# Up to eight MLP tiles ahead of their second matmul, kept in the spectral buffers while these are free, and three after that; the opening's order on two engines written out to tile 10; the splits of w2 placed among the other work

## The chip, the cores and the metric

The kernel runs on one core of a Trainium2 chip. The metric is the device time of one execution in microseconds (us). The core has a matmul engine (PE; its weight loads are PEld), a vector engine (DVE), a scalar engine (ACT), a general engine (POOL) and a queue that issues the DMAs (SP). Each engine works through its own list of instructions in order and waits at an instruction until what that one needs is there.

## The reference, cut to what is computed

```python
x = A_x                                        # [1, 2048, 512]
xn = layernorm(x, axis=-1)
X = rfft2(xn, axes=(-2, -1)) * (w_r + 1j*w_i)  # 2048 x 257 weights
y = irfft2(X, s=(2048, 512))
h = einsum("bsd,df->bsf", xn, w1) + b1         # 512 -> 1792
act = h * tanh(softplus(h))                    # Mish
return x + y + einsum("bsf,fd->bsd", act, w2)  # 1792 -> 512
```

All is float32. The kernel keeps that precision by splitting each float32 operand into a float16 "high" and "low" part and making three float16 matmuls of each product (high-high, high-low, low-high).

## The kernel before

**Two streams of work.** The MLP is cut into 4 groups `g` of 512 rows and 14 tiles `f` of 128 hidden columns. A tile goes *up* (`mlp_up`, L707: 12 matmuls into `ph_g_f`; ACT makes `hb` = Mish of it; then `split` makes the tile `a_g_f` in two halves, the high one on ACT and the low one on DVE) and *down* (`mlp_down`, L734: 12 matmuls `pa` with the tile `a_g_f` and the part f//2 of w2). Each up and each down is one *half-tile*; there are 112. After the last down of a group `mlp_end` adds x to the four sums (DVE `m`, L757; x comes by the DMAs `xr`, two at a time). The spectral branch is a 2-D transform over 16 sub-tiles `s2` = 4g+s of 128 rows, forward, times the weights, and back. `mlp_all` is a generator: `b(n)` takes the next n half-tiles from it and so lays MLP work between pieces of the other branch.

**The opening** (up to `spread`) loads x, w1, w2, normalises group 0, measures and splits w1 (seven parts, `split_w1`), measures w2 (`norm_w2`, seven parts; parts 0 to 2 on ACT, 3 to 6 on DVE) and sums these over partitions on POOL (`w2_scale`), which gives the scale for `split_w2`. Part c of w2 is split in place: it is written into block c and read from block c+1, so part c+1 can be split only after part c.

**The spread** (L913 to L956) then runs 21 slots. In a slot stand pieces of the spectral branch and then one `b(1)`. For groups 1 to 3 the pieces are `stats` (DVE statistics; then the reciprocal root `rs` by 14 small operations on POOL), `norm` (DVE `xs`; ACT high part of `xh`; POOL low part of `xh`), `transpose` (PE `pt`, 4 matmuls on the high and 4 on the low part, copied out by DVE and ACT to `xnT`) and `s1_forward` (PE `psS1`, three matmuls; ACT `bc`; DVE `bt` twice; ACT high and POOL low part of `y1`; DMA to `d_y1`). From slot 13 on, `prep_spectral` also loads the spectral weights once (`wm`) to find their largest value (DVE `mxw`). Of w2 one part is split in every second slot.

**After that** `stream_a` runs the second stage of the forward transform (`psP`), the spectrum (`psD`), and the way back (`psA`, a round trip by DMA through `d_a`, `psT`) for four chunks, with half-tiles laid between by weight up to half-tile 100; then `s1_inverse` (`psY`) with the last 12 half-tiles.

**What sets the order.** The code is recorded; a scheduler of the framework then orders each engine's list from the recorded dependencies and its own estimates. `tc.issue_after` and `in_order` add dependencies that only order. `behind()` puts pieces after the last up's and down's instructions.

**Buffers.** Each tag is a ring. Tiles `a` have a ring of 3, so a tile waits until the tile three before it in the ring has gone down; in group 0 the tiles 3 to 10 lie instead in the buffers "z" and "u" (four tiles each), which before held parts of w1 and later hold spectral data. `hb` has a ring of 3; `ph` and `pt` share a ring of 2 PSUM banks (tag "h"); `psS1` has 2 banks, `pa` 4; `bt`, `bc` and `xs` have 2, `y1` 3, `xh` 4 and the large load buffers ("big") 5.

`LAG`, `E_UP` and the condition in `mlp_all` (L767) set how far ups run ahead of downs: 11 ups first, then an up only when fewer than 2 tiles are ahead, or after two downs.

## Time and profile before

| | us |
|---|---|
| three runs, median | 422.77 (422.55 to 424.7) |
| the profiled execution, its own time | 423.4 |
| its span, first to last instruction | 421.6 |

The profiled execution's time is 1.8 us more than its span. In the profile a time is counted from the span's start; a row of a group gives busy time, the mean of one, and the idle time of the engine just before it with what ended it. "PEclk" is the share of full speed at which PE's clock ran. The mean of one matmul (383 ns for 512 columns) is longer than the distance of two that follow each other, since they overlap.

### The profile page before, as it was taken

The page shows a single profiled execution, that of the slowest core. Times are in us where ns is not written, and L with a number is a line of the kernel's source. Part 1 is how long each engine was busy: PE and PEld are TensorE (multiplying, and loading weights), DVE is VectorE, ACT ScalarE, POOL GpSimd, SP SyncE. Part 2 cuts the span into 40 slices and gives each one's busy share as a digit, 9 for nine tenths or more (in the row PEclk, how much of TensorE's full clock was granted, in tenths as well). Part 3 has the DMA queues.
Part 4 walks back from the last instruction along what each step waited for, and adds up shares of the span by engine and source line. Part 5 has one row for each costly group of instructions (what it writes and reads, how often), then busy time and mean ns, then how long its engine had stood idle before and what let it go on. Part 6 is the DMA issues. An engine that isn't in the chain of part 4 may idle for free.

```text
span 421.6 us, 6597 instructions
## 1 busy us (share of the span) xinstructions
PE 391.7 (93%) x2485; PEld 193.2 (46%) x2485; DVE 251.2 (60%) x520; ACT 202.1 (48%) x325; POOL 70.7 (17%) x103
## 2 busy tenths in 40 slices
PE   8889987999959799979999998999999899989996
PEld 3434333444424345445545464444555454543442
DVE  5979957872296313983495743776245955333435
ACT  4869737662244124644536453546435455342120
POOL 0000075874055100000112000111001120031000
PEclk9999998999997899989999999999999999999999
DMA  8995122353063994154514816315435111445675
GB/s 286 368 398 223 52 67 82 101 157 119 1 233 120 242 231 151 33 130 110 181 51 151 220 31 177 122 54 147 104 81 172 50 50 51 129 148 174 200 241 206
DMA packets 50816, 61.61 MB, mean 146 GB/s; under 512 B 3921, under 2 KB 36177, under 8 KB 50529
## 3 DMA queue, kind: packets, MB, share of 16 engines
q1 hardware_dynamic: 50784, 61.20, 47.6%
q8 instruction: 19, 0.31, 0.3%
q14 instruction: 13, 0.10, 0.1%
HBM read 44.38 MB, written 16.78 MB: 145 GB/s over the span
## 4 chain that ended last, share of the span: by engine, by line
PE 48%; DVE 15%; issue 10%; DMA 10%; ACT 7%; POOL 5%; SPq 4%; POOLq 0%; DVEq 0%; ACTq 0%
PE ph L716 18%; PE pa L87 6%; PE pa L83 6%; PE pa L86 6%; DMA ai<-d_a 3%; PE psP L512 3%; PE psD L536 2%; DMA cTt<-in_cT_dram 2%; DMA xr<-in_x_dram 2%; DVE m L757 1%; SPq L358 1%; ACT a L331 1%; DMA d_a<-at 1%; DVE w2r L332 1%; POOL y L126 1%
## 5 line engine op out<-in xcount | busy, mean ns | idle before, releaser
L716 PE MATMUL ph<-xnT,w1t 128*128 128x512 f16 x672 | 157.2, 383 | 2.4 <-ACT hb L721 2.3
L716 PEld LDWEIGHTS <-w1t 128*128 128x128 f16 x672 | 64.9, 99 | 80.1 <-issue 7.0
L83 PE MATMUL pa<-w2r,a 128*128 128x512 f16 x224 | 86.3, 386 | 3.4 <-DVE m L757 3.4
L87 PE MATMUL pa<-w2r,a 128*128 128x512 f16 x224 | 86.7, 387 | 2.0 <-DVE a L332 2.0
L86 PE MATMUL pa<-w2r,a 128*128 128x512 f16 x224 | 86.6, 387 | 1.0 <-DVE w2r L332 1.0
L332 DVE SCALAR_TENSOR_TENSOR a<-hb,sc_a,a 128x512 f16<-128x512 f32 x56 | 42.8, 767 | 72.2 <-ACT a L331 72.0
L721 ACT ACTIVATE hb<-ph,b1t,sc_exp 128x512 f32<-128x512 f32 x56 | 43.2, 773 | 69.9 <-PE ph L716 69.9
L126 POOL TENSOR_TENSOR tt<-bt_t,tt 128x512 f16<-128x512 f32 x16 | 19.2, 1206 | 216.1 <-DMA d_a<-at 115.7
L331 ACT ACTIVATE a<-hb,sc_a 128x512 f16<-128x512 f32 x56 | 40.1, 719 | 14.2 <-PE pa L87 13.0
L87 PEld LDWEIGHTS <-a 128*128 128x128 f16 x224 | 22.3, 99 | 31.2 <-issue 3.5
L86 PEld LDWEIGHTS <-a 128*128 128x128 f16 x224 | 22.3, 99 | 29.8 <-issue 6.7
L83 PEld LDWEIGHTS <-a 128*128 128x128 f16 x224 | 22.1, 99 | 25.8 <-issue 1.7
L126 POOL TENSOR_TENSOR y<-bt_s,y 128x512 f16<-128x512 f32 x16 | 20.2, 1266 | 30.0 <-ACT y L125 30.0
L331 ACT ACTIVATE u<-r,sc_u 128x512 f16<-128x512 f32 x16 | 11.6, 722 | 24.6 <-DVE r L616 13.8
L197 PE MATMUL pt<-cMt,xh 128*128 128x128 f16 x128 | 11.8, 225 | 10.8 <-ACT xh L190 3.4
L125 ACT CAST tt<-bt_t 128x512 f16<-128x512 f32 x16 | 9.9, 618 | 15.1 <-DVE bt_t L123 14.2
L805 DVE SCALAR_TENSOR_TENSOR m<-psY,sc_k,m 128x512 f32<-128x512 f32 x12 | 8.6, 747 | 14.2 <-PE psY L87 14.2
L197 PEld LDWEIGHTS <-xh 128*128 128x128 f16 x128 | 8.3, 99 | 18.5 <-ACT xh L190 5.3
L671 DVE SCALAR_TENSOR_TENSOR at<-psA,at 128x512 f16<-128x512 f32 x16 | 10.7, 686 | 8.9 <-ACT at L670 8.9
L525 DVE SCALAR_TENSOR_TENSOR z<-psP,z 128x512 f16<-128x512 f32 x16 | 10.8, 688 | 8.8 <-ACT z L524 8.6
L122 DVE SCALAR_TENSOR_TENSOR bt_t<-psT,bc_t 128x256 f32<-128x256 f32 x16 | 6.8, 423 | 14.0 <-ACT bc_t L118 12.6
L524 ACT ACTIVATE z<-psP 128x512 f16<-128x512 f32 x16 | 9.3, 593 | 11.9 <-PE psP L512 11.6
(146 smaller groups left out, 526.5 us busy)
## 6 DMA issues: line engine op xcount, KB each, us to landing
wt<-in_wt_dram SPq DMA_DIRECT2D x32, 256.0 KB
x<-in_x_dram SPq DMA_DIRECT2D x8, 512.0 KB
d_y<-y SPq DMA_DIRECT2D x16, 256.0 KB
wm<-in_wt_dram SPq DMA_DIRECT2D x8, 512.0 KB
yt<-d_y SPq DMA_DIRECT2D x16, 256.0 KB
d_a<-at SPq DMA_DIRECT2D x32, 128.0 KB
ai<-d_a SPq DMA_DIRECT2D x16, 256.0 KB
d_t<-tt SPq DMA_DIRECT2D x16, 256.0 KB
```

The lines of the kernel that those rows point to most:

```text
L83: first = nc.tensor.matmul(ps, stat(0), mov(0), start=start, stop=False)
L86: nc.tensor.matmul(ps, stat(0), mov(1), start=False, stop=False)
L87: return nc.tensor.matmul(ps, stat(1), mov(0), start=False, stop=stop)
L126: nc.gpsimd.tensor_sub(out[:, :, 1, :], tv, out[:, :, 0, :])
L197: nc.tensor.transpose(pt[:, h, dc, :], xh[:, h, dc * P : (dc + 1) * P], ident)
L331: hi = nc.scalar.activation(dst_h, src, AF.Copy, scale=scale)
L332: lo = nc.vector.scalar_tensor_tensor(dst_l, src, scale, dst_h, op0=ALU.mult, op1=ALU.subtract)
L512: first = nc.tensor.matmul(ps[64 * be : 64 * be + 64, pr, k, :], yt[:, 2 * pr + be, hs, k, :], c_p2[:, k, v, hm, :], start=t == 0, stop=t ...
L525: nc.vector.scalar_tensor_tensor(zl, psv, 2.0**-15, zh, op0=ALU.mult, op1=ALU.subtract)
L671: nc.vector.scalar_tensor_tensor(at[:, :, 1, :], psv, 2.0**-15, at[:, :, 0, :], op0=ALU.mult, op1=ALU.subtract)
L716: last_mm = nc.tensor.matmul(ph, w1t[:, hs, dc, f * P : (f + 1) * P], xnT[g][:, hm, dc, :], start=n == 0, stop=n == 11)
L721: nc.scalar.activation(hb, ph, AF.Mish, bias=b1t[:, f : f + 1], scale=s_exp[k])
```

## The change

It does this:

- **Lead.** While `sc["ahead"]` is set (until slot 15), an up is taken when fewer than 8 tiles are ahead (`LEAD`); after that when fewer than 3 are (`LAG` was 2). The first 11 ups stay. New conditions (`home`, `free`) let an up be recorded only if its buffer's earlier tile has gone down.
- **Where tiles lie.** Tiles are counted through (14g+f). Of each twelve, four lie in the ring `a` (now 4) and eight in "z" and "u", as long as `ahead` holds; before, these two took tiles 3 to 10 of group 0 only.
- **hb.** The ring is 2 (was 3); the first two tiles use the ring of `xs`.
- **Opening.** Tiles 0 and 1 are split later, together with tile 2. ACT's and DVE's order is written out by `in_order` from `bias_max` to tile 10. `norm_w2` 3 to 6 stand earlier, and `split_w2(0)` stands in the opening.
- **Spread.** Parts 1 to 6 of w2 stand in slots 1, 4, 7, 10, 13 and 15, first in the slot. There are 24 slots; `wm` loads run two steps ahead of their `mxw`.

```diff
-LAG = 2
+LAG = 3
+LEAD = 8
...
-        for c in range(8):
-            t = big.tile([P, 1024], F32, tag="big", name=f"wm_{c}")
-            nc.sync.dma_start(t, wt_any[:, 1024 * c : 1024 * c + 1024])
-            nc.vector.tensor_reduce(mxw[:, c : c + 1], t, axis=AX.X, op=ALU.max, apply_absolute_value=True)
+        wm = []
+        for c in range(10):
+            if c < 8:
+                wm.append(big.tile([P, 1024], F32, tag="big", name=f"wm_{c}"))
+                nc.sync.dma_start(wm[c], wt_any[:, 1024 * c : 1024 * c + 1024])
+            if c > 1:
+                nc.vector.tensor_reduce(
+                    mxw[:, c - 2 : c - 1], wm[c - 2], axis=AX.X, op=ALU.max, apply_absolute_value=True
+                )
...
-        hb = mp.tile([P, 512], F32, tag="hb", name=f"hb_{g}_{f}", bufs=3)
+        if g == 0 and f < 2:
+            hb = tp.tile([P, 512], F32, tag="ix", name=f"hb_{g}_{f}", bufs=2)
+        else:
+            hb = mp.tile([P, 512], F32, tag="hb", name=f"hb_{g}_{f}", bufs=2)
...
-        if g == 0 and 2 < f < E_UP:
-
-            if f in (3, 7):
-                sc["ea"] = tp.tile([P, 4, 2, 512], F16, tag="zu"[f // 4], name=f"a_{g}_{f}")
-            a = sc["ea"][:, (f - 3) % 4]
+        r = (NFC * g + f) % 12
+        if sc["ahead"] and r > 3:
+
+            if r % 4 == 0:
+                sc["ea"] = tp.tile([P, 4, 2, 512], F16, tag="zu"[r // 8], name=f"a_{g}_{f}")
+            a = sc["ea"][:, r % 4]
         else:
-            a = mp.tile([P, 2, 512], F16, tag="a", name=f"a_{g}_{f}", bufs=3)
+            a = mp.tile([P, 2, 512], F16, tag="a", name=f"a_{g}_{f}", bufs=4)
+            in_a.append(NFC * g + f)
         acts[g, f] = a
-        last["up"] = (last_mm.ins, *split(a[:, 0, :], a[:, 1, :], hb, sc["a"]))
+        wait.append((a, hb))
+        if g == 0 and f < 2:
+            return
+        if g == 0 and f in (2, 3):
+            split_w1(f)
+        while wait:
+            a, hb = wait.pop(0)
+            last["up"] = (last_mm.ins, *split(a[:, 0, :], a[:, 1, :], hb, sc["a"]))
...
-            if up < len(tiles) and (up < E_UP or up - down < LAG or (n_down == 2 and up - down > LAG)):
+            lag = LEAD if sc["ahead"] else LAG
+
+            home = sc["ahead"] and up % 12 > 3
+            free = down >= up - up % 4 - 8 if home else len(in_a) < 4 or in_a[-4] < down
+            if free and up < len(tiles) and (up < E_UP or up - down < lag or (n_down >= 2 and up - down > lag)):
...
-    with tc.issue_after(ends[0]), tc.issue_after(ends[1]):
+    with tc.issue_after(ends[0]), tc.issue_after(ends[1]), in_order(mybir.EngineType.Activation, mybir.EngineType.DVE):
+
...
-    b(2)
-    split_w1(2)
-    with behind():
-        norm_w2(0)
...
+        b(4)
+        norm_w2(3)
+        norm_w2(4)
+        b(1)
+        split_w1(4)
+        norm_w2(5)
+        b(1)
         norm_w2(0)
...
+        split_w2(0)
+        b(1)
+        split_w1(6)
+        b(1)
...
-        if w2_left and done[0] % 2:
-            split_w2(w2_left.pop(0))
...
+    for c in range(1, 7):
+        slots[(1, 4, 7, 10, 13, 15)[c - 1]].insert(0, (split_w2, c))
+
+    for k in range(13, 23):
+        slots[k].append((next, maxima, None))
     for k in sorted(slots):
+        if k == 15:
+            sc["ahead"] = False
```

**Place 1: ACT in the opening**, between the first two Mish tiles (`hb_0_0`, `hb_0_1`) and the tile `a_0_3`. In the rows `w1t<-w1s` is a part of w1 being split and `w2r,q2` a `norm_w2`. Before, and then with the change:

```order
L721 ACTIVATE hb_0_1_370<-ph_0_1_357,b1t_94,sc_exp_0_252 128x512
L331 ACTIVATE w1t_92<-w1s_2_106,sc_w1_1_325 128x4x256
L331 ACTIVATE a_0_0_354<-hb_0_0_352,sc_a_337 128x512
L331 ACTIVATE a_0_1_372<-hb_0_1_370,sc_a_337 128x512
L428 ACTIVATE w2r_93,q2_95<-w2r_93 128x1024
L721 ACTIVATE hb_0_2_391<-ph_0_2_378,b1t_94,sc_exp_0_252 128x512
L331 ACTIVATE w1t_92<-w1s_2_106,sc_w1_1_325 128x4x256
L331 ACTIVATE a_0_2_393<-hb_0_2_391,sc_a_337 128x512
L721 ACTIVATE hb_0_3_413<-ph_0_3_400,b1t_94,sc_exp_0_252 128x512
L331 ACTIVATE w1t_92<-w1s_4_109,sc_w1_1_325 128x4x256
L331 ACTIVATE a_0_3_415<-hb_0_3_413,sc_a_337 128x512
```

```order
L731 ACTIVATE hb_0_1_368<-ph_0_1_355,b1t_94,sc_exp_0_252 128x512
L731 ACTIVATE hb_0_2_384<-ph_0_2_371,b1t_94,sc_exp_0_252 128x512
L332 ACTIVATE w1t_92<-w1s_2_106,sc_w1_1_325 128x4x256
L332 ACTIVATE a_0_0_354<-hb_0_0_352,sc_a_337 128x512
L332 ACTIVATE a_0_1_370<-hb_0_1_368,sc_a_337 128x512
L332 ACTIVATE a_0_2_386<-hb_0_2_384,sc_a_337 128x512
L731 ACTIVATE hb_0_3_408<-ph_0_3_395,b1t_94,sc_exp_0_252 128x512
L332 ACTIVATE w1t_92<-w1s_2_106,sc_w1_1_325 128x4x256
L332 ACTIVATE a_0_3_410<-hb_0_3_408,sc_a_337 128x512
L731 ACTIVATE hb_0_4_432<-ph_0_4_419,b1t_94,sc_exp_1_327 128x512
```

`hb_0_2` moved ahead of the first part of w1, and the `norm_w2` that stood ahead of it moved further back (behind `a_0_5`).

**Place 2: DVE around the statistics of group 1** (`BN_STATS`, then `ve`), after the last of the first eleven tiles; `w2r<-w2r` is a `split_w2`, `qt`, `pn` and `sc_w2` are the small operations of `w2_scale`. Before, and then with the change:

```order
L173 BN_STATS st_1_530<-x_1_0_122 128x6
L317 TENSOR_SCALAR qt_w2_483<-qt_w2_483 128x1
L173 BN_STATS st_1_530<-x_1_0_122 128x6
L319 TENSOR_SCALAR pn_w2_487<-qt_w2_483 128x1
L173 BN_STATS st_1_530<-x_1_1_124 128x6
L325 TENSOR_SCALAR sc_w2_489<-pn_w2_487 128x1
L439 SCALAR_TENSOR_TENSOR s_out_491<-p2_H_335,pn_w2_487 128x1
L173 BN_STATS st_1_530<-x_1_1_124 128x6
L175 BN_AGGR mv_1_531<-st_1_530 128x2 x4
L332 SCALAR_TENSOR_TENSOR a_0_7_508<-hb_0_9_582,sc_a_337,a_0_7_508 128x512
L177 TENSOR_SCALAR ve_1_540<-mv_1_531 128x4
L332 SCALAR_TENSOR_TENSOR w2r_93<-w2r_93,sc_w2_489 128x1024
```

```order
L333 SCALAR_TENSOR_TENSOR w2r_93<-w2r_93,sc_w2_525 128x1024
L333 SCALAR_TENSOR_TENSOR a_0_8_514<-hb_0_9_544,sc_a_337,a_0_8_514 128x512
L333 SCALAR_TENSOR_TENSOR w1t_92<-w1s_6_112,sc_w1_1_325,w1t_92 128x4x256
L333 SCALAR_TENSOR_TENSOR a_0_8_514<-hb_0_10_563,sc_a_337,a_0_8_514 128x512
L174 BN_STATS st_1_567<-x_1_0_122 128x6 x2
L174 BN_STATS st_1_567<-x_1_1_124 128x6 x2
L176 BN_AGGR mv_1_568<-st_1_567 128x2 x4
L333 SCALAR_TENSOR_TENSOR w2r_93<-w2r_93,sc_w2_525 128x1024
L178 TENSOR_SCALAR ve_1_577<-mv_1_568 128x4
L123 SCALAR_TENSOR_TENSOR bt_s1_0_629<-psS1_0_622,bc_s1_0_627 128x4x64
L124 SCALAR_TENSOR_TENSOR bt_s1_0_629<-psS1_0_622,bc_s1_0_627 128x4x64
L123 SCALAR_TENSOR_TENSOR bt_s1_1_654<-psS1_1_647,bc_s1_1_652 128x4x64
```

The statistics and `ve_1` stood ahead of the first `split_w2`; now two `split_w2`, the last part of w1 and the tiles 9 and 10 stand ahead of `ve_1`, and the operations of `w2_scale` have gone ahead of all this.

**Place 3: DVE between groups 2 and 3 of the spread**: `xs_12` begins the normalisation of group 3, `a_1_n` is the low half of tile n of group 1. Before, and then with the change:

```order
L123 SCALAR_TENSOR_TENSOR bt_s1_10_1109<-psS1_10_1102,bc_s1_10_1107 128x4x64
L332 SCALAR_TENSOR_TENSOR a_1_0_1134<-hb_1_0_1132,sc_a_337,a_1_0_1134 128x512
L287 COPY xnT_2_969<-pt_11_1137 128x4x128
L122 SCALAR_TENSOR_TENSOR bt_s1_11_1155<-psS1_11_1148,bc_s1_11_1153 128x4x64
L123 SCALAR_TENSOR_TENSOR bt_s1_11_1155<-psS1_11_1148,bc_s1_11_1153 128x4x64
L452 TENSOR_REDUCE mxw_1115<-wm_1_1161 128x1
L187 TENSOR_SCALAR xs_12_1177<-x_3_0_908,mv_3_1041,rs_3_1075 128x512
L452 TENSOR_REDUCE mxw_1115<-wm_2_1181 128x1
L187 TENSOR_SCALAR xs_13_1197<-x_3_0_908,mv_3_1041,rs_3_1075 128x512
```

```order
L333 SCALAR_TENSOR_TENSOR a_1_1_1120<-hb_1_1_1118,sc_a_337,a_1_1_1120 128x512
L288 COPY xnT_2_997<-pt_10_1125 128x4x128
L333 SCALAR_TENSOR_TENSOR w2r_93<-w2r_93,sc_w2_525 128x1024
L123 SCALAR_TENSOR_TENSOR bt_s1_10_1143<-psS1_10_1136,bc_s1_10_1141 128x4x64
L124 SCALAR_TENSOR_TENSOR bt_s1_10_1143<-psS1_10_1136,bc_s1_10_1141 128x4x64
L288 COPY xnT_2_997<-pt_11_1164 128x4x128
L123 SCALAR_TENSOR_TENSOR bt_s1_11_1182<-psS1_11_1175,bc_s1_11_1180 128x4x64
L124 SCALAR_TENSOR_TENSOR bt_s1_11_1182<-psS1_11_1175,bc_s1_11_1180 128x4x64
L333 SCALAR_TENSOR_TENSOR a_1_2_1205<-hb_1_2_1203,sc_a_337,a_1_2_1205 128x512
L188 TENSOR_SCALAR xs_12_1211<-x_3_0_932,mv_3_1069,rs_3_1103 128x512
L333 SCALAR_TENSOR_TENSOR w2r_93<-w2r_93,sc_w2_525 128x1024
L456 TENSOR_REDUCE mxw_1149<-wm_0_1150 128x1
L188 TENSOR_SCALAR xs_13_1231<-x_3_0_932,mv_3_1069,rs_3_1103 128x512
```

Ahead of `xs_12` stood tile 0 of group 1, on the ring of 3; now tiles 0 and 1 and a part of w2 are done before, and the last tile ahead of it is `a_1_2`, which lies in "z".

On PE the first down now follows tile 10 directly (before, `psS1_0` and `psS1_1` stood ahead of it), the transposes `pt_4` and `pt_5` stand after four and five downs (before two and three), and at `psS1_15` 18 ups and 13 downs have been issued, 17 and 14 before. Before, six downs and one up stood between `psS1_11` and `pt_12`, and the four transposes of group 3 then came with one up among them; now each two transposes that follow each other have one to three half-tiles between them, through groups 2 and 3.

More of the change, by code (lines that the diff above doesn't have):

```diff
@@ L702, in ip_unit @@
         )
-    macc, yacc, last = {}, {}, {}
+    macc, yacc, last, wait, in_a = {}, {}, {}, [], []
+    sc["ahead"] = True
     def mlp_up(g, f, acts):
@@ L882, in spectral_mlp_kernel @@
         act_scale()
-    b(2)
-    split_w1(2)
-    with behind():
-        norm_w2(0)
-    b(1)
-    with behind():
-        norm_w2(3)
-    split_w1(3)
-    b(1)
-    with behind():
-        norm_w2(1)
-        norm_w2(4)
-    b(1)
-    split_w1(4)
-    b(1)
-    with behind():
-        norm_w2(2)
-        norm_w2(5)
-    split_w1(5)
-    b(1)
-    with behind():
-        norm_w2(6)
+        b(4)
[5 more added lines that the diff above has]
+        b(1)
+        norm_w2(0)
+        norm_w2(6)
+        b(1)
+        split_w1(5)
+        b(1)
+        norm_w2(1)
+        norm_w2(2)
+        b(1)
         w2_scale()
-    b(1)
-    split_w1(6)
-    b(1)
-    w2_left = list(range(7))
+        split_w2(0)
+        b(1)
+        split_w1(6)
+        b(1)
     maxima = prep_spectral()
@@ L937, in matrices @@
         nc.sync.dma_start(cMt[:, :O_ID], cM[:, :O_ID])
-    slots = {k: [] for k in range(21)}
+    slots = {k: [] for k in range(24)}
     for s in range(4):
@@ L952, in spectral_mlp_kernel @@
     slots[19].append((load_it,))
-    for k in range(13, 21):
-        slots[k].append((lambda: next(maxima),))
+    for c in range(1, 7):
+        slots[(1, 4, 7, 10, 13, 15)[c - 1]].insert(0, (split_w2, c))
+    for k in range(13, 23):
+        slots[k].append((next, maxima, None))
     for k in sorted(slots):
+        if k == 15:
+            sc["ahead"] = False
         spread(*(lambda f=f, a=a: f(*a) for f, *a in slots[k]))
-    for _ in w2_left:
-        split_w2(_)
     for _ in maxima:
-        b(1)
+        pass
     for be in range(2):
```

## The prediction

> **What bounds the kernel now.** I read the page first (busy shares, slices), then the busy time by stage, then who PE waits for.
>
> ```profile
> PE 391.7 (93%) x2485; PEld 193.2 (46%) x2485; DVE 251.2 (60%) x520; ACT 202.1 (48%) x325; POOL 70.7 (17%) x103
> PE   8889987999959799979999998999999899989996
> ```
>
> PE is busy 93% of the span, and what it lacks lies in the first 40% of the slices, where its clock is down too, as the next view shows.
>
> ```profile
> core 0: us, PE busy (x) PEld busy (x) DVE busy (x) ACT busy (x) POOL busy (x), PEclk, DMA share, GB/s
> 17.30:57.40 40.10, 36.70 (x168) 16.45 (x169) 33.50 (x68) 32.34 (x47) 5.61 (x15) 1.00 0.57 213
> 57.40:76.00 18.60, 13.72 (x72) 6.23 (x71) 14.01 (x21) 10.92 (x18) 11.89 (x12) 0.91 0.36 106
> 76.00:117.40 41.40, 41.33 (x221) 19.71 (x219) 21.38 (x46) 18.32 (x32) 20.67 (x39) 1.00 0.28 86
> 117.40:136.00 18.60, 13.95 (x73) 6.25 (x73) 15.32 (x24) 8.46 (x17) 9.69 (x10) 0.82 0.55 179
> 136.00:158.70 22.70, 20.55 (x86) 8.57 (x84) 6.96 (x14) 5.30 (x8) 2.67 (x8) 0.92 0.94 237
> 158.70:385.70 227.00, 218.77 (x1647) 115.23 (x1646) 131.24 (x286) 111.56 (x184) 19.25 (x16) 0.99 0.39 112
> ...
> 65.00:68.90 3.90, 0.93 (x5) 0.30 (x4) 3.35 (x4) 2.33 (x3) 1.05 (x2) 1.00 0.22 67
> 70.00:73.20 3.20, 3.20 (x9) 1.16 (x8) 3.20 (x7) 3.07 (x6) 0.88 (x2) 0.50 0.26 82
> 120.00:124.00 4.00, 1.85 (x14) 0.64 (x12) 4.00 (x7) 2.15 (x6) 1.16 (x1) 1.00 0.92 314
> 126.00:128.00 2.00, 1.66 (x7) 0.86 (x8) 2.00 (x2) 0.10 (x1) 0.74 (x2) 0.50 0.44 138
> 180.00:184.00 4.00, 2.73 (x10) 1.02 (x10) 4.00 (x10) 2.71 (x4) 0.00 (x0) 0.82 1.03 233
> 184.00:188.00 4.00, 3.90 (x76) 3.02 (x75) 2.89 (x6) 1.19 (x2) 0.00 (x0) 0.75 0.13 27
> ```
>
> The columns: stretch, its length, busy time of PE, PEld, DVE, ACT, POOL, then PE's clock. I cut where PE's work changes: the opening to `ph_0_11` (57.4), group 1 of the spread (76), group 2 (117.4), group 3 (136), the turn to group 1's downs (158.7, first `psP`), `stream_a` (385.7). A stage's loss is its idle time plus length x (1 - PEclk):
>
> - 17.3 to 57.4: 40.10 - 36.70 = **3.4**.
> - 57.4 to 76: 4.9 idle and 18.6 x 0.09 = 1.7 by clock: **6.6**.
> - 76 to 117.4: 0.1.
> - 117.4 to 136: 4.65 idle and 18.6 x 0.18 = 3.35: **8.0**.
> - 136 to 158.7: 2.15 idle and 22.7 x 0.08 = 1.8: **4.0**.
>
> Together 22.0 us before the first `psP`. The work units come from distances of starts:
>
> ```profile
> 17.32 10.54 PE L716 MATMUL ph<-xnT,w1t 128*128 128x512 f16 x48
> 98.51 0.61 PE L197 MATMUL pt<-cMt,xh 128*128 128x128 f16 x8
> 98.95 0.38 PE L83 MATMUL psS<-xh,cTt 128*128 128x512 f16 x1
> ...
> 99.60 0.38 PE L83 MATMUL pa<-w2r,a 128*128 128x512 f16 x1
> ```
>
> 48 matmuls of an up end 10.54 us after the first starts, 0.216 apart, so a half-tile is 2.59; a `psS1` is 0.65 (98.95 to 99.60) and a `pt` 0.44. To the first `psP` the lists hold 39.2 half-tiles before and 38.8 with the change, beside the same 16 `psS1` and 12 `pt`, and from there to the first `psY` as much more: PE's work is only moved. So the question is which of the 22 us go.
>
> ```profile
> PE pt L197 <- ACT xh L190: 3.4, 3, 2.0
> PE pa L83 <- DVE m L757: 3.4, 4, 1.3
> PE pt L197 <- POOL xh L191: 3.1, 5, 1.1
> PE pt L197 <- ACT hb L721: 3.0, 1, 3.0
> PE ph L716 <- ACT hb L721: 2.3, 2, 2.0
> PE pa L87 <- DVE a L332: 2.0, 1, 2.0
> PE psT L83 <- DMA ai<-d_a: 3.6, 6, 1.3
> ```
>
> PE waits mostly for the transposes' inputs (3.4 + 3.1 + 3.0).
>
> **The change part by part.** I walk each engine's list with these durations (successive ones overlap by some 0.07):
>
> ```profile
> L126 POOL TENSOR_TENSOR y<-bt_s,y 128x512 f16<-128x512 f32 x16 | 20.2, 1266 | 30.0 <-ACT y L125 30.0
> L332 DVE SCALAR_TENSOR_TENSOR a<-hb,sc_a,a 128x512 f16<-128x512 f32 x56 | 42.8, 767 | 72.2 <-ACT a L331 72.0
> L331 ACT ACTIVATE a<-hb,sc_a 128x512 f16<-128x512 f32 x56 | 40.1, 719 | 14.2 <-PE pa L87 13.0
> L332 DVE SCALAR_TENSOR_TENSOR w2r<-w2r,sc_w 128x1024 f16<-128x1024 f32 x7 | 10.6, 1508 | 3.0 <-ACT w2r L331 3.0
> L331 ACT ACTIVATE w1t<-w1s,sc_w 128x1024 f16<-128x1024 f32 x6 | 6.9, 1144 | 2.2 <-DVE sc_w L325 2.2
> L332 DVE SCALAR_TENSOR_TENSOR w1t<-w1s,sc_w,w1t 128x1024 f16<-128x1024 f32 x6 | 7.7, 1278 | 2.0 <-ACT w1t L331 2.0
> ```
>
> *Opening (place 1).* The up of tile 2 ends at 17.3 + 3 x 2.59 = 25.1. Now `hb_0_2` runs at once (25.3 to 26.0); before it started at 29.0 behind a w1 part, two tiles and a `norm_w2`, and `ph_0_4`, which needs its bank, lost 2.0. Next late is w1's part 2: high 26.0 to 27.05, low to 28.35, wanted at 28.1 by `ph_0_4`'s third matmul: 0.25. After that PE finds everything over 1 us early (part 3 at 31.9 for 33.1, part 4 at 36.8 for 38.3, `hb_0_8` at 42.5 for 43.5). `norm_w2` ends on ACT at 41.9, the POOL sum and six DVE operations give `sc_w2` at 44.9, `split_w2(0)` is there at 46.0 and 47.25 for the first down at 46.1 and 47.2. I take 0.6 in place of 3.4 (0.3 to 3.4). The hb ring of 2 costs nothing, as `a_0_(n-2)` is split over 2 us before `hb_0_n` starts; without that cover it costs 0.7 a tile.
>
> *Group 1 (place 2).* Here the change also moves something the wrong way. DVE reaches the statistics at 50.3 behind tile 10, and `ve_1` comes at 54.3, not 50.0.
>
> ```profile
> 45.15 0.47 POOL L306 PARTITION_ALL_REDUCE qs_w<-q  x1 [20.46 <-ACT a L331]
> 52.25 0.49 POOL L145 TENSOR_SCALAR rr<-ve 128x4 int32<-128x4 int32 x1 [6.63 <-DVE bt_s L123]
> 59.28 0.25 POOL L166 TENSOR_SCALAR rs<-rr 128x4 f32<-128x4 f32 x1
> 62.20 2.13 POOL L126 TENSOR_TENSOR y<-bt_s,y 128x512 f16<-128x512 f32 x1
> ...
> 61.15 2.17 DVE L332 SCALAR_TENSOR_TENSOR w2r<-w2r,sc_w 128x1024 f16<-128x1024 f32 x1
> ```
>
> The chain on POOL took 7.3 from 52.25 to 59.5, of which 2.3 are two `y1` in it; so 4 to 5: `rs_1` at 58.3 to 59.3. Three `y1` now stand ahead of `xh_4` (3.5), and where a w2 split on DVE meets a `y1` on POOL each took 1 longer (2.17 and 2.13). `xh_4` is whole at 63 to 64.4. PE comes to `pt_4` at 46.1 + 5 x 2.59 + 4 x 0.65 + 0.2 = 61.9, so it waits 1.1 to 2.5. The 3.0 of `pt_5` before was for `hb_0_11` behind the serial w2 splits on ACT; now `hb_0_11` ends at 56.3, 11 us early. Taken: 2.7 in place of 6.6; from 1.1 to 4.5, when the clock falls as after 65.9.
>
> The clock: after the wait of 3.0 it ran at 0.50 for 3.2 us (70.0 to 73.2); after the 2.0 at 27.9 it stayed at 1.00. The Trainium skill (TensorE: Matmul & The Clock Gate, Part 1) says that a free-running window of about 3.4 us in which PE idles halves the clock, so that a given gap may or may not trip it; the trace agrees in the size, though a 3.0 gap sufficed. By that rule the 2.5 here costs 0 or 1.7.
>
> When the chain may start is read in two ways. The row at 52.25 blames DVE's `bt`. By that label the chain now starts at 55.7, `pt_4` waits up to 3.9 and the clock surely falls: 5.6 for this group. But `ve` was ready at 50.2, and 6.6 us lie between POOL's end at 45.6 and 52.25. The Trainium skill (GPSIMD Engine Reference, 2.1 Instruction dispatch) gives about 6 us for loading other POOL code, with no row of its own; the trace's 6.6 fits that. By it the load now runs from 42.5 to 49.2, under the opening, and the chain starts with `ve`.
>
> *Groups 2 and 3 (place 3).*
>
> ```profile
> 107.58 0.78 ACT L721 ACTIVATE hb<-ph,b1t,sc_exp 128x512 f32<-128x512 f32 x1 [8.09 <-PE ph L716]
> 112.81 0.72 ACT L331 ACTIVATE a<-hb,sc_a 128x512 f16<-128x512 f32 x1 [4.46 <-PE pa L87]
> 113.57 0.75 DVE L332 SCALAR_TENSOR_TENSOR a<-hb,sc_a,a 128x512 f16<-128x512 f32 x1 [16.12 <-ACT a L331]
> ```
>
> Before, ACT waited 8.1 for the up of tile 1 and 4.5 for a place in the ring of 3, DVE 16.1 for ACT; PE meanwhile used up six downs, and group 3's normalisation, queued behind on DVE, came when nothing was left to cover it: the 8.0. Now `a_1_0` finds its place free since 58, and each transpose has half-tiles ahead of it. With a w2 split, copies, `bt` and `xs` in list order, low parts of `xh_8` to `xh_11` are there at 84.3, 86, 91, 92 and PE asks at 84.4, 88, 91.8, 95.5; of `xh_12` to `xh_15` at 104.4, 107, 108.2, 110.6 against 104.4, 108, 112, 115.6. Two of eight are level. Engine load allows it: DVE has some 82 us of work in 102. I take 1.5 in place of 8.1, 0 to 8. The `wm` loads, which SP issues in order between the `y1` stores, move with the buffers they wait for; their result is first needed by the spectrum tens of us later, so nothing.
>
> *The turn.* The last down of group 0 ends near 120. Two `m` are done by then, the other two wait for `xr`, issued when the first are through; before, these cost most of 3.4 (the `m` row) and the clock 1.8. Between now stand four sums of other tiles (3 us) and five matmuls. Taken 1.5 in place of 4.0 (0 to 4).
>
> *stream_a.* The psD pair that followed the first by 2 us of PE work stands 9 us behind now; with it goes the crowding on DVE behind the 2.05 wait for `a` (and 1.7 by clock at 180 to 188), and the third tile ahead covers the rest. Against that, from the first chunk's `psA` to its `psT` 8.3 us of work stand, not 9.3, and the last `psT` comes 1.1 closer: about 2.4 more waiting for `ai` (0 to 5). Net -1.3.
>
> Sum: (22.0 - 0.6 - 2.7 - 1.5 - 1.5) = 15.7 (the 0.1 of group 2 is in the 1.5), and 1.3: **17.0 us less**. From the profiled execution's 423.4 this gives 406.4; the median of the runs is 0.6 below that execution, so **406**.
>
> **The rivals.**
>
> *Contention (413).* The same POOL, DVE and ACT work is pressed into 17 us less. POOL has about 50 us between `ve_1` and the last `y1`, in 66. The pair at 61 to 64 shows 1 us each when both read together. If each of groups 2 and 3's eight transposes comes 0.9 late, 7 more: 413. For it: two are level already. Against: the lead over the other six is 1.7 to 5 us. The Trainium skill (GPSIMD Engine Reference, 1. Specifications) says that POOL shares its memory interface with DVE; it makes this likelier, and the trace agrees with the 2.13.
>
> *It doesn't do what it says (421).* The lead at the end of the spread is 5, before 3, and if the queue, not the lead, sets the time of `xh`, the same waits come at other transposes. Only the opening's 2 to 3 us stay. Against: the 16.1 on DVE hangs on the ring.
>
> *Slower (427).* Repeated short waits keep the clock at half. Group 3's four transposes cost 8.0, 2.0 each, half of it clock (120 to 128: busy 1.85 of 4.0, then 0.50). If all twelve fare so, 24, with 0.6 and 1.5 elsewhere, 26 in place of 22: 427. It decides once a wait of 1 us recurs within some 4 us of work; transposes now stand 3.7 us apart, so that could be, but needs POOL or DVE as the bound all through.
>
> *Better (400).* All at the low ends: 0.3 + 1.1 + 0 + 0, and no more `psT` waits.
>
> **How the numbers follow.** Forecast 403 to 410: 0.60; contention 410 to 417: 0.21; it doesn't do it: 0.07, mostly within 0.5%; slower: 0.04; better: 0.08. The range leaves out the slower end and the best tenth: 400.5 to 416. Half a per cent, 2.1 us, is about what a measurement of this kernel tells from no change. Faster 0.90, same 0.05, slower 0.05.
>
> **What would show it.** No idle PE of 2 us at `ph_0_4`; one wait at `pt_4` of 1 to 2.5; no long idle time of DVE for ACT in the spread; `pt_12` to `pt_15` without waits over 1; the first `psP` near 141; PEclk 1.0 from 76 to the first `psP`. Wrong would make it: waits at most of `pt_6` to `pt_15`, a late `rs_1` (after 60), or a clock at half past 65.

## The result and the profile after

| | before | changed |
|---|---|---|
| median of the runs | 422.66 (420.69 to 424.7) | 408.85 (406.99 to 411.29) |
| the profiled execution | 423.4 | 408.1 |
| its span | 421.6 | 406.3 |
| first `psP` | 158.7 | 144.1 |
| first `psY` | 385.7 | 370.1 |

The ratio is 0.9676, with a 95% interval of 0.9605 to 0.9747. The forecast was 406 (from 400.5 to 416), so the time is in the range and 2.9 us above the point; against the profiled execution the sum was 1.7 us too low (406.4 for 408.1).

The page of the changed kernel first: its line of busy time, PE's slices and PE's clock.

```profile
PE 384.7 (95%) x2485; PEld 191.2 (47%) x2485; DVE 250.6 (62%) x520; ACT 202.8 (50%) x325; POOL 68.2 (17%) x103
PE   8899997999998999999997999999999899998996
PEclk9999998999999999999999999999999999999999
```

PE rose from 93% to 95% of a shorter span. Slices 12 and 14, at 5 and 7 tenths before, are now full (a slice is 10.2 us). Dents are left in the seventh, with the clock at 8 tenths, in the 13th, and in the 22nd, where sums of group 1 are waited for.

Next the busy time by stage of the changed kernel (stretch, its length, busy time of PE, PEld, DVE, ACT, POOL, PE's clock, DMA share, GB/s). The cuts are near those of before in the work: opening, group 1, groups 2 and 3 together, the turn, `stream_a`, and last the 3.8 us behind the longest wait.

```profile
17.50:61.70 44.20, 42.83 (x196) 19.06 (x197) 35.26 (x69) 33.95 (x49) 5.57 (x19) 1.00 0.51 192
61.70:80.00 18.30, 15.72 (x88) 7.51 (x87) 14.12 (x27) 10.22 (x18) 14.14 (x23) 0.91 0.45 139
80.00:128.30 48.30, 47.26 (x265) 23.13 (x264) 36.00 (x65) 28.53 (x49) 28.11 (x40) 1.00 0.49 156
128.30:144.10 15.80, 13.85 (x65) 5.98 (x65) 4.38 (x11) 3.00 (x4) 0.38 (x1) 1.00 1.04 260
144.10:370.10 226.00, 217.71 (x1650) 114.41 (x1649) 132.88 (x287) 113.38 (x186) 19.07 (x16) 1.00 0.40 113
66.60:70.40 3.80, 3.78 (x13) 1.55 (x14) 3.80 (x6) 1.49 (x3) 3.49 (x3) 0.55 0.78 247
```

A stage's loss is again its idle time plus length x (1 - clock):

| stage | before | forecast | measured |
|---|---|---|---|
| opening | 3.4 | 0.6 | 44.20 - 42.83 = 1.4 |
| group 1 | 6.6 | 2.7 | 2.6 idle + 18.3 x 0.09 = 4.2 |
| groups 2 and 3 | 8.1 | 1.5 | 48.30 - 47.26 = 1.0 |
| turn | 4.0 | 1.5 | 15.80 - 13.85 = 1.95 |
| together | 22.1 | 6.3 | 8.6 |

So 13.5 us went before the first `psP`, of 15.8 that were forecast. The first `psP` comes 14.6 us earlier, since 0.4 half-tiles (1 us) of PE's list also moved behind it. `stream_a` became 1.0 shorter all the same (227.0 to 226.0), and the tail 0.3 longer: 14.6 + 1.0 - 0.3 = 15.3, the difference of the spans. The 1.0 is of this one profile: in a second one of the same kernel (after_again below) `stream_a` took 228.4.

What PE waits for in the changed kernel (total, times, longest):

```profile
PE pa L84 <- DVE m L776: 5.4, 6, 1.3
PE pt L198 <- POOL xh L192: 3.5, 3, 2.5
PE psT L84 <- DMA ai<-d_a: 2.4, 5, 1.3
PE pa L84 <- ACT w2r L332: 0.8, 1, 0.8
PE ph L723 <- DVE w1t L333: 0.5, 1, 0.5
```

The 2.0 of `ph` for `hb`, the 3.0 of `pt` for `hb` and the 2.0 of `pa` for DVE's `a` are gone. The waits for `xh` fell from 3.4 + 3.1 to 3.5, of which 2.5 is one wait. New at the top are the sums `m` (5.4, before 3.4).

The one long wait in order of time, from POOL's, DVE's and PE's timelines of the changed kernel (start, duration, engine, line, operation; in brackets the idle time before and what ended it):

```profile
52.23 2.46 DVE L174 BATCH_NORM_STATS2 st<-x 128x6 f32<-128x512 f32 x4
54.89 1.25 DVE L333 SCALAR_TENSOR_TENSOR w2r<-w2r,sc_w 128x1024 f16<-128x1024 f32 x1
56.06 0.16 DVE L178 TENSOR_SCALAR ve<-mv 128x4 f32<-128x4 f32 x1
...
56.33 0.20 POOL L146 TENSOR_SCALAR rr<-ve 128x4 int32<-128x4 int32 x1 [12.32 <-DVE ve L178]
60.28 0.25 POOL L167 TENSOR_SCALAR rs<-rr 128x4 f32<-128x4 f32 x1
60.51 2.27 POOL L127 TENSOR_TENSOR y<-bt_s,y 128x512 f16<-128x512 f32 x2
63.19 2.08 POOL L127 TENSOR_TENSOR y<-bt_s,y 128x512 f16<-128x512 f32 x1 [0.41 <-ACT y L126]
65.23 1.33 POOL L192 TENSOR_TENSOR xh<-xs,xh 128x512 f16<-128x512 f32 x1
...
66.62 0.40 PE L198 MATMUL pt<-cMt,xh 128*128 128x128 f16 x4 [2.45 <-POOL xh L192]
```

Read it upwards from the last row. PE stands 2.45 us at the low half of `pt_4`. `xh_4`'s low part ends at 66.56; three `y1` stand ahead of it on POOL (60.5 to 65.2). `rs_1` is there at 60.5, fourteen small operations behind `ve_1` at 56.2. And `ve_1` is late because DVE came to the statistics at 52.2, and then took a part of w2 (1.25) between `mv` and `ve`.

### The profile page after: what moved, and what is told of

It is laid out like the page before. It is cut to its first block, busy times and chain, and to the rows that moved or that the text cites. A ratio compares the mean times of both kernels' runs of the same rounds, so it can differ in the third digit from the quotient of the medians.

```text
span 406.3 us, 6601 instructions
## 1 busy us (share of the span) xinstructions
PE 384.7 (95%) x2485; PEld 191.2 (47%) x2485; DVE 250.6 (62%) x520; ACT 202.8 (50%) x325; POOL 68.2 (17%) x103
## 4 chain that ended last, share of the span: by engine, by line
PE 44%; DVE 21%; DMA 13%; ACT 8%; issue 6%; POOL 5%; SPq 2%; POOLq 0%; DVEq 0%; ACTq 0%
PE ph L723 16%; PE pa L84 6%; PE pa L88 6%; PE pa L87 6%; DMA ai<-d_a 4%; PE psP L518 3%; PE psD L542 3%; DMA xr<-in_x_dram 3%; DVE m L776 2%; DMA d_a<-at 2%; DVE xs L188 2%; ACT a L332 2%; DMA w1s<-in_w_dram 2%; DVE w1t L333 2%; ACT hb L731 1%
## 5 line engine op out<-in xcount | busy, mean ns | idle before, releaser
L723 PE MATMUL ph<-xnT,w1t 128*128 128x512 f16 x672 | 155.1, 379 | 0.6 <-DVE w1t L333 0.5
L84 PE MATMUL pa<-w2r,a 128*128 128x512 f16 x224 | 84.9, 381 | 6.2 <-DVE m L776 5.4
L87 PE MATMUL pa<-w2r,a 128*128 128x512 f16 x224 | 85.4, 381 | 0.1
L88 PE MATMUL pa<-w2r,a 128*128 128x512 f16 x224 | 85.1, 381 | 0.0
L84 PEld LDWEIGHTS <-a 128*128 128x128 f16 x224 | 22.1, 98 | 26.6 <-issue 2.1
L127 POOL TENSOR_TENSOR y<-bt_s,y 128x512 f16<-128x512 f32 x16 | 19.6, 1230 | 10.2 <-ACT y L126 10.2
L192 POOL TENSOR_TENSOR xh<-xs,xh 128x512 f16<-128x512 f32 x12 | 14.8, 1240 | 8.3 <-ACT xh L191 8.3
L123 DVE SCALAR_TENSOR_TENSOR bt_t<-psT,bc_t 128x256 f32<-128x256 f32 x16 | 6.8, 422 | 14.9 <-ACT bc_t L119 13.5
L126 ACT CAST y<-bt_s 128x512 f16<-128x512 f32 x16 | 9.9, 617 | 12.1 <-DVE bt_s L124 5.9
L198 PE MATMUL pt<-cMt,xh 128*128 128x128 f16 x128 | 10.8, 220 | 4.8 <-POOL xh L192 3.5
```

The costliest lines, as they stand in the source:

```text
L84: first = nc.tensor.matmul(ps, stat(0), mov(0), start=start, stop=False)
L87: nc.tensor.matmul(ps, stat(0), mov(1), start=False, stop=False)
L88: return nc.tensor.matmul(ps, stat(1), mov(0), start=False, stop=stop)
L126: nc.scalar.copy(out[:, :, 0, :], tv)
L127: nc.gpsimd.tensor_sub(out[:, :, 1, :], tv, out[:, :, 0, :])
L192: nc.gpsimd.tensor_sub(xh[:, 1, :], xs, xh[:, 0, :])
```

## The experiments

The runs were made in three sets of four, in the order of the table, each set on a chip of its own. Each set has its own runs of the kernel before (medians 421.24, 421.17 and 423.71), and each ratio is against the runs of its own set. The medians of this one kernel differ by up to 2.5 us between the sets, so it is the ratios that compare across them.

| run | median us | ratio, 95% interval | first `psP` | first `psY` |
|---|---|---|---|---|
| no_lead | 413.95 | 0.9814 (0.9766 to 0.9862) | 145.5 | 373.2 |
| lag2 | 408.85 | 0.9696 (0.9651 to 0.9740) | 142.0 | 370.3 |
| w2_old | 409.54 | 0.9705 (0.9643 to 0.9767) | 143.5 | 372.0 |
| open_old | 414.01 | 0.9813 (0.9772 to 0.9854) | 145.7 | 374.6 |
| before_free | 413.92 | 0.9810 (0.9753 to 0.9867) | 137.7 | 374.5 |
| stats_early | 407.85 | 0.9679 (0.9614 to 0.9744) | 141.9 | 368.3 |
| xr_ix | 406.59 | 0.9645 (0.9594 to 0.9697) | 142.4 | 368.8 |
| stats_xr | 406.03 | 0.9631 (0.9567 to 0.9694) | 141.1 | 368.0 |
| x_in_m | 402.93 | 0.9524 (0.9462 to 0.9585) | 141.1 | 365.1 |
| x_in_m_stats | 402.01 | 0.9502 (0.9440 to 0.9564) | 139.4 | 363.8 |
| x_in_m_y1 | 401.59 | 0.9491 (0.9409 to 0.9574) | 140.9 | 364.1 |
| after_again (the changed kernel) | 408.70 | 0.9677 (0.9606 to 0.9748) | 143.6 | 372.0 |

### What made groups 2 and 3 wait: the lead, or the place?

**no_lead** takes the lead away and leaves the buffers:

```diff
-LAG = 3
-LEAD = 8
+LAG = 2
+LEAD = 2
```

> The changed kernel with LAG = LEAD = 2, so the ups follow the rule of before; the ring of 4, the tiles kept in z and u, the opening and the places of the w2 splits stay. Theory 1 (the order counts: the six tiles of lead are what stands between the transposes of groups 2 and 3): the waits of group 3 come back, 6 to 8 us there, some at the turn, 1 in the stretch behind: 416 to 420. Theory 2 (the buffers count: what cost group 3 was the place in the ring of 3): the 16.1 us of DVE idle time do not come back and the time stays within 3 us of 409. Theory 3 (opening and w2 splits alone made the gain): no change at all, 408 to 410.

The waits of group 3 did not come back, nor did the idle time of DVE; the time rose by 5 us all the same. By stage (groups 2 and 3; turn; `stream_a`):

```profile
80.00:128.30 48.30, 46.93 (x262) 22.83 (x261) 35.86 (x64) 28.57 (x49) 29.17 (x53) 1.00 0.47 152
128.30:145.50 17.20, 14.71 (x69) 6.38 (x67) 4.20 (x10) 3.87 (x6) 0.38 (x1) 1.00 0.97 246
145.50:373.20 227.70, 218.58 (x1645) 114.20 (x1644) 131.40 (x287) 111.16 (x184) 19.17 (x16) 0.99 0.39 112
```

Groups 2 and 3 lose 1.4, against 1.0 in the changed kernel. So theory 1, that the lead is what stands between the transposes, falls: with no lead there is still a half-tile between each two transposes of group 3. Theory 2 is right on the place and wrong on the time.

**before_free** goes the other way. To the kernel before it adds only the rule that an up whose place isn't free is not put in the lists:

```diff
         else:
             a = mp.tile([P, 2, 512], F16, tag="a", name=f"a_{g}_{f}", bufs=3)
+            in_a.append(NFC * g + f)
...
-            if up < len(tiles) and (up < E_UP or up - down < LAG or (n_down == 2 and up - down > LAG)):
+            free = 2 < up < E_UP or len(in_a) < 3 or in_a[-3] < down
+            if free and up < len(tiles) and (up < E_UP or up - down < LAG or (n_down == 2 and up - down > LAG)):
```

> The kernel before with one rule added: an up whose tile lies in the ring of 3 is taken only when the tile three before it in the ring has gone down (else a down is taken). Nothing else changes. Theory 1 (what cost group 3 was a tile that stood in ACT's and DVE's lists ahead of the norms and waited for its place): the 16.1 us of DVE idle time and the waits of pt_12 to pt_15 go, the first psP comes 6 to 9 us earlier, 413 to 416. Theory 2 (more places are needed, the rule alone only moves the wait to PE, which comes to downs whose tiles aren't there yet): 418 to 424. Theory 3 (the spacing of the transposes by lead counts): 420 to 423.

Theory 1 holds. Its stages are group 1, groups 2 and 3 (76 to 117, all but the last transpose), the turn and `stream_a`:

```profile
57.40:76.00 18.60, 12.18 (x72) 5.68 (x70) 13.98 (x21) 10.89 (x18) 11.92 (x12) 1.00 0.36 106
76.00:117.00 41.00, 40.92 (x238) 20.45 (x237) 31.27 (x59) 21.64 (x40) 29.78 (x53) 1.00 0.56 170
117.00:137.70 20.70, 16.21 (x75) 6.95 (x75) 9.90 (x20) 6.45 (x11) 3.09 (x4) 0.92 0.85 253
137.70:374.50 236.80, 231.07 (x1715) 120.64 (x1714) 134.04 (x289) 116.37 (x190) 19.27 (x16) 1.00 0.38 108
```

Groups 2 and 3 lose 0.1, with a ring of 3, no lead and everything else as before; the 8.0 of before is gone. One half-tile stands between each two transposes of group 3 here as well: with no tile holding up the norms, the transposes come one to a slot, as the code has them. The turn is worse than before, 4.5 idle and 1.7 by clock, of which 3.9 is one wait for a sum `m`. The time falls to 413.92, a little over half of the gain. The first `psP` comes 21 us earlier than before (137.7), of which over half is MLP work that now stands behind it (PE is busy 12.3 us more in `stream_a`), and the first `psY` 11.2. The medians give 7.3, since the execution profiled here was the fastest of its four (412.17) and the one of before, at 423.4, a slow one.

What the lead is worth is seen between no_lead and **lag2** (`LAG = 2`, `LEAD = 8`), which differ in `LEAD` alone:

> The changed kernel with LAG = 2 and LEAD = 8: two tiles ahead after slot 15 in place of three. Theory 1 (the third tile covers little, the gain lies before the first psP): 409 to 411, the stretch from the first psP to the first psY 226 to 228 us. Rival (the third tile is what keeps PE fed in that stretch and at the turn): 413 or more, with waits of pa for DVE's a of 2 us as before.

```profile
128.30:142.00 13.70, 13.57 (x65) 5.86 (x62) 3.79 (x11) 2.88 (x4) 0.38 (x1) 1.00 1.05 277
142.00:370.30 228.30, 219.03 (x1646) 114.45 (x1646) 131.51 (x287) 111.08 (x184) 19.16 (x16) 0.99 0.39 112
```

Their intervals do not overlap: 8 tiles of lead are worth about 5 us in the medians, 2.9 in the spans (410.4 and 407.5). The profile shows it at the turn: 0.13 idle here, 2.5 in no_lead. With the lead the last down of group 0 comes later (it ends at 124.1, in no_lead at 120.9), and PE comes later to the sums that are late. The third tile at the end (`LAG`) makes no difference in time that the runs can tell (0.9696 and 0.9676). Without it the first `psP` comes 2 us earlier than in the changed kernel and `stream_a` takes 2.3 longer (228.3 against 226.0), but that this is the work of `LAG` isn't shown: 1.7 of it is a clock of 0.57 from 216 to 220, and in after_again, with the third tile, the clock fell there as well and `stream_a` took 228.4.

### The opening and the places of the w2 splits

**open_old** has the opening of before, and part 0 of w2 in slot 0:

```diff
-        if g == 0 and f < 2:
-            return
-        if g == 0 and f in (2, 3):
-            split_w1(f)
...
-    with tc.issue_after(ends[0]), tc.issue_after(ends[1]), in_order(mybir.EngineType.Activation, mybir.EngineType.DVE):
-
+    with tc.issue_after(ends[0]), tc.issue_after(ends[1]):
...
-        b(4)
+    b(2)
+    split_w1(2)
+    with behind():
+        norm_w2(0)
+    b(1)
+    with behind():
         norm_w2(3)
...
+    slots[0].insert(0, (split_w2, 0))
```

> The changed kernel with the opening of before (no written order, norm_w2 and w1 parts in the old places, tiles 0 and 1 split at once), and part 0 of w2 in slot 0. Theory 1 (the opening is worth its own idle time): the 2.0 at ph_0_4 comes back and part 0 of w2 comes late at the first down, 2 to 4 more: 411 to 413. Rival (the opening also made room on ACT for group 1): the 3 us wait for hb_0_11 comes back as well with the clock behind it: 414 to 418.

It is at 414.01, 5 us above the changed kernel. Opening, a part of it, group 1 and turn:

```profile
18.00:61.70 43.70, 40.52 (x178) 17.81 (x179) 34.39 (x69) 32.31 (x47) 6.99 (x19) 0.96 0.53 196
28.40:34.00 5.60, 3.59 (x12) 1.34 (x11) 4.24 (x6) 5.60 (x9) 0.00 (x0) 0.79 1.04 409
61.70:80.00 18.30, 16.06 (x90) 7.66 (x89) 14.22 (x32) 11.44 (x21) 12.66 (x22) 0.91 0.45 130
126.00:145.75 19.75, 15.74 (x62) 6.22 (x60) 5.06 (x11) 3.00 (x4) 0.38 (x1) 0.83 0.83 215
```

The opening loses 3.2 idle and 1.7 by clock (1.4 in the changed kernel): the 2.0 at `ph_0_4` is back, and this time the clock fell behind it (0.79 from 28.4 to 34). Group 1 loses 2.2 idle and 1.6 by clock, no more than the changed kernel, and the wait for `hb_0_11` did not come back; so the rival's mechanism is not there. The rest is the turn: 4.0 idle, 3.7 of it one wait for a sum `m`, for which DVE in turn waited 3.5 for a load of x, and the clock at 0.83. The size was the rival's, the cause another one that neither theory had. Why the opening's order is felt as late as the turn isn't shown.

**w2_old** splits parts 1 to 6 of w2 as before:

```diff
+    w2_left = list(range(1, 7))
...
+        if w2_left and done[0] % 2:
+            split_w2(w2_left.pop(0))
         b(1)
...
-    for c in range(1, 7):
-        slots[(1, 4, 7, 10, 13, 15)[c - 1]].insert(0, (split_w2, c))
```

> The changed kernel with parts 1 to 6 of w2 split as before, in every second slot behind its pieces. Theory 1 (it only decides what stands ahead of the first norm): xh_4 1 to 2 us earlier or later, 407 to 412. Rival (the spacing of the splits is what keeps ACT and DVE free for the transposes): waits at most of pt_5 to pt_11, 413 to 418.

409.54: no difference that the runs can tell, so this part of the change is worth nothing measurable by itself.

### The late `ve_1`, and POOL

**stats_early** puts the statistics of group 1 into the opening:

```diff
         split_w2(0)
         b(1)
+        early = stats(1, xs[1])
         split_w1(6)
```

> The changed kernel with the statistics of group 1 in the opening, ahead of part 6 of w1 on DVE. Theory (the wait of 2.45 at pt_4 and the clock of 0.55 behind it are the late ve_1, handed on by 14 POOL operations): ve_1 at about 52.8 in place of 56.2, rr right behind it, xh_4 3 us earlier, both go: 4 us less, 404 to 406. Rival (POOL's queue of y1 or the low part sets xh_4, or POOL isn't ready before 56): the wait stays above 1.5 and the time within 1.5 us of 409.

`ve_1` came 3.6 us earlier (52.64), as meant, but `pt_4` still waited 1.65. The rows of POOL, DVE and PE in this kernel:

```profile
52.75 1.14 POOL L146 TENSOR_SCALAR rr<-ve 128x4 int32<-128x4 int32 x1 [8.81 <-DVE ve L178]
53.98 0.57 POOL L152 TENSOR_TENSOR rt<-rr 128x4 f32<-128x4 f32 x1
54.63 1.12 POOL L156 TENSOR_TENSOR rq<-rt,ve 128x4 f32<-128x4 f32 x1
55.83 0.19 POOL L157 TENSOR_SCALAR rq<-rq 128x4 f32<-128x4 f32 x1
58.64 0.25 POOL L167 TENSOR_SCALAR rs<-rr 128x4 f32<-128x4 f32 x1
...
52.55 1.28 DVE L333 SCALAR_TENSOR_TENSOR w1t<-w1s,sc_w,w1t 128x1024 f16<-128x1024 f32 x1
53.74 0.74 DVE L333 SCALAR_TENSOR_TENSOR a<-hb,sc_a,a 128x512 f16<-128x512 f32 x1
54.41 1.28 DVE L333 SCALAR_TENSOR_TENSOR w2r<-w2r,sc_w 128x1024 f16<-128x1024 f32 x1
...
65.44 0.40 PE L198 MATMUL pt<-cMt,xh 128*128 128x128 f16 x4 [1.65 <-POOL xh L192]
```

POOL's operation began 0.1 behind `ve_1`, as in the changed kernel. But its first three operations took 1.14, 0.57 and 1.12 where these took 0.20, 0.20 and 0.20 in the changed kernel: at the same time DVE split the last part of w1, a tile `a` and a part of w2. So `rs_1` came 1.6 us earlier and not 3.6, and the three `y1` still stood ahead of `xh_4`. The wait was 0.8 shorter, and the clock stayed at full speed behind it, which is another 1.7 in this profile. The median, 407.85, can't be told from the changed kernel's: the rival's outcome.

### The turn: sums that wait for x

Sums 3 and 4 of each group need x, loaded into a ring of two; so their loads are issued only behind sums 1 and 2. The rows of DVE, SP and PE in the changed kernel:

```profile
124.93 1.40 DVE L776 SCALAR_TENSOR_TENSOR m<-pa,s_out,xr 128x512 f32<-128x512 f32 x2
130.90 0.75 DVE L776 SCALAR_TENSOR_TENSOR m<-pa,s_out,xr 128x512 f32<-128x512 f32 x1 [1.53 <-DMA xr<-in_x_dram]
132.59 0.75 DVE L776 SCALAR_TENSOR_TENSOR m<-pa,s_out,xr 128x512 f32<-128x512 f32 x1 [0.94 <-DMA xr<-in_x_dram]
...
126.61 1.00 SPq L775 DMA_DIRECT2D xr<-in_x_dram  x2
...
131.70 0.38 PE L84 MATMUL pa<-w2r,a 128*128 128x512 f16 x1 [1.06 <-DVE m L776]
133.40 0.38 PE L84 MATMUL pa<-w2r,a 128*128 128x512 f16 x1 [0.89 <-DVE m L776]
```

The loads are issued at 126.6, among those of the spectral weights, and the sums are at 130.9 and 132.6; PE waits 1.06 and 0.89 for their banks. **xr_ix** gives the two loads of group 0 the ring of `xs`:

```diff
-                xr = mp.tile([P, D], F32, tag="xr", name=f"xr_{g}_{s}")
+                if g == 0 and s > 1:
+                    xr = tp.tile([P, D], F32, tag="ix", name=f"xr_{g}_{s}", bufs=2)
+                else:
+                    xr = mp.tile([P, D], F32, tag="xr", name=f"xr_{g}_{s}")
```

> The changed kernel with x for the third and fourth sum of group 0 (xr 2 and 3) in the ring of xs, so that these loads need not wait for the first two sums. Theory 1 (the turn's 1.06 and 0.89 are the late xr loads, among wt loads): both waits go, first psP at 142, 2 us less, 406 to 408. Rival (as with LAG = 2, where the first psP came 2 us earlier and the first psY at the same time: the stretch behind the first psP has slack against PE's lead and gives it back): first psP 2 us earlier, first psY the same, 408 to 410.

Both waits went, the first `psP` came at 142.4 and the first `psY` at 368.8, 1.7 and 1.3 earlier than in the changed kernel. The median, 406.59, is theory 1's too; but the changed kernel did not run in this set, and the intervals of the two ratios overlap, so that nothing was given back is only shown by x_in_m below. **stats_xr** has both edits:

> Both edits, early statistics of group 1 and xr 2 and 3 of group 0 in the ring of xs. If each removes its own waits and nothing is given back behind: 6 us less than the changed kernel, 402 to 404. If the stretch behind the first psP gives it back: 406 to 409.

406.03, not the 402 to 404 expected. By the ratios stats_early gains nothing on the changed kernel, xr_ix 1.3 us and both together 1.9; the runs can't tell that from a plain sum.

**x_in_m** does it for three groups: x is loaded into the buffer of the sums, which the group's last up has freed, and summed in place.

```diff
+        if g < 3 and f == NFC - 1:
+            macc[g] = cp.tile([P, 4, D], F32, tag=f"xnT{g}", name=f"m_{g}")
+            for s in range(4):
+                nc.sync.dma_start(macc[g][:, s, :], xv[:, 4 * g + s, :])
...
-                xr = mp.tile([P, D], F32, tag="xr", name=f"xr_{g}_{s}")
-                nc.sync.dma_start(xr, xv[:, 4 * g + s, :])
+                xr = m[:, s, :]
```

> The changed kernel with the x rows of groups 0 to 2 loaded straight into the buffer of the sums (m) as soon as the last up of the group has freed it, and summed in place; no xr for these. Theory (the waits of pa for m, 5.4 us of PE in the profile of the changed kernel, 1.95 of them at the turn, are the loads xr 2 and 3, issued only after sums 1 and 2): all of them go, first psP at 142, the stretch from there to psY 3 us shorter, 403 to 405. Rival (what the sums wait for is covered by other waits, ai above all, and the stretch gives it back): 406.5 to 409.

It ran at 402.93, 5.8 below the changed kernel on the same chip (408.70). Turn, `stream_a` and the head of the list of PE's waits:

```profile
129.00:141.10 12.10, 12.10 (x57) 5.32 (x55) 4.49 (x10) 3.00 (x4) 0.38 (x1) 1.00 1.06 274
141.10:365.10 224.00, 218.98 (x1658) 115.30 (x1658) 132.67 (x287) 113.51 (x186) 19.58 (x16) 1.00 0.41 115
...
PE pt L198 <- POOL xh L192: 3.5, 3, 2.5
PE psT L84 <- DMA ai<-d_a: 2.1, 4, 0.9
```

The turn is without loss, the idle time of `stream_a` fell from 8.3 to 5.0, and one wait for `m` of 0.5 is left of 5.4. So nearly all that PE lost to the late loads was a gain still to be had, and none of it was given back. Whether the lead, which brings PE later to these sums, is still worth its 5 us with x loaded in this way was not run.

**x_in_m_stats** adds the early statistics:

> The same and the early statistics of group 1: 1.7 less than x_in_m if the two add (402 to 403.5), the same as x_in_m if the early statistics only move the wait.

402.01: 0.9 less, where 1.7 was expected, and the intervals overlap. **x_in_m_y1** also moves group 0's first stage behind the transposes of groups 1 and 2:

```diff
-        slots[1 + s].append((s1_forward, 0, s, xh[0, s]))
+        slots[(9, 10, 15, 16)[s]].append((s1_forward, 0, s, xh[0, s]))
```

> The same again, with the first stage of the forward transform of group 0 (psS1_0 to 3 and their bt, bc, y1) in slots 9, 10, 15 and 16 in place of 1 to 4. Theory (three y1 on POOL and their bt on DVE stand ahead of xh_4, 3.5 us in the sum of the prediction and 5.2 in the profile): no wait at pt_4, PE's clock 1.0 throughout, 1.5 to 2.5 less than x_in_m_stats. Rival (the later y1 crowd group 2 or 3 on POOL): waits over 1 at pt_11 to pt_15 and no gain, or a loss of up to 3.

401.59, the fastest median, but not apart from 402.01. The wait at `pt_4` fell from 1.65 in x_in_m_stats to 1.04, and the one at the first transpose of group 2 rose from 1.00 to 2.35:

```profile
62.57 0.40 PE L198 MATMUL pt<-cMt,xh 128*128 128x128 f16 x4 [1.04 <-POOL xh L192]
86.80 0.40 PE L198 MATMUL pt<-cMt,xh 128*128 128x128 f16 x4 [2.35 <-POOL xh L192]
```

So POOL's work ahead of an `xh` does set these waits, and moving it moves the wait: the rival, at an earlier transpose than it named and without its loss.

## Why the prediction was right

**Opening (0.6, measured 1.4).** `ph_0_4` found its bank, as forecast. The wait for w1's part 2 was 0.5, not 0.25. Part 0 of w2 came 0.8 late, where the walk had it level: the last `norm_w2` ended on ACT at 43.4, not 41.9, and so `sc_w2` was there 1.5 us later than in the walk. The mechanism was right; this term was mis-sized. (The row of 48 matmuls from which the prediction takes a half-tile's 2.59 is four ups, not one; the 2.59 is right.)

**Group 1 (2.7, measured 4.2).** PE's wait of 2.45 lies at the upper end of the 1.1 to 2.5 given. `ve_1` came at 56.2, not at 54.3, since DVE reached the statistics 1.9 later; the 4.0 from there to `ve_1`, a part of w2 included, are those of the walk. PE came to `pt_4` 1.9 late as well (63.8), so this delay hardly counts. The term that was mis-sized is the three `y1` ahead of `xh_4`: 4.7 us (60.5 to 65.2), not 3.5, one of them 2.08 beside a split of w2. The clock took the worse branch, 0.55 for 3.8 us, 1.7.

Of the two readings of when POOL's chain may start, the label (DVE's `bt`) falls: POOL began at 56.33, 0.1 behind `ve_1`, and the first `bt` behind `ve_1` ended only at 56.9. The Trainium skill (GPSIMD Engine Reference, 2.1 Instruction dispatch) gives about 6 us for loading other POOL code. The trace agrees as far as it goes: POOL had stood idle for 12.3 us since 44.0, and no part of a load shows behind `ve_1`; that a load ran in that time isn't shown.

**Groups 2 and 3 (1.5, measured 1.0).** The 16.1 us of DVE for ACT went, and no wait over 0.8 us is left. The step has two reasons in it: that the tile finds its place free, and that each transpose has half-tiles ahead of it. before_free shows that the first is the root: a tile that waits in ACT's and DVE's lists for its place holds up every norm behind it, and without it the 8.0 goes. The second does not come from the lead, since in before_free and no_lead the half-tiles stand between the transposes too. What the first would be worth without the second is open; no run has the one without the other.

**The turn (1.5, measured 1.95).** The size was right; the reason given, work between the sums, only hides what xr_ix and x_in_m took away, the loads of x that are issued too late.

**`stream_a` (1.3 less; measured 1.0 less with 1 us more of PE's work in it).** The 2.05 for `a` went. The 2.4 more of waiting for `ai` did not come: it fell from 3.6 to 2.4. Against it stood waits for `m`, which the sum did not have for this stage: three that end at 216.7 to 220.0 and one of 1.26 at 317, together 3.5. Two wrong terms cancelled, so that the net came out is luck; in after_again the stage took 228.4, which is longer than before.

**The signs.** Most came as named, but the first `psP` stands at 144.1, not near 141, and two of the signs of being wrong appeared: `rs_1` after 60 (60.5) and a clock at half past 65 (0.55 from 66.6 to 70.4). Both belong to group 1, whose price in the sum had room for them up to 4.5.

**The rivals.** Contention (413): groups 2 and 3 lost 1.0, not 8.5; what there is of it stands in group 1, at the `y1` of 2.08. "It doesn't do what it says" (421) was half right in its reason, that the lead does not set the time of `xh`, and wrong in its time, since the ring and the rule do. Slower (427): the clock fell once in this profile, three times in after_again.

## What to carry to other kernels

Where engines work through their lists in order, don't record an operation before its buffer's earlier tile is used up: a rule of a few lines that checks for it (before_free) gave half of what this large change gave, and idle time of an engine that is not the bottleneck (16.1 us of DVE behind ACT) was the sign. Then look for loads that wait for a small ring at each change of groups: loading into the buffer that the sum will have anyway took 5.8 us off and needed no new space. And when a gain comes early in a kernel, compare a later milestone too: in before_free 21 us at the first `psP` are 11 at the first `psY`. Profile the same kernel twice before explaining a us or two of a stage, since `stream_a` took 226.0 and 228.4 in two profiles of one kernel.
